# Fewer, larger loads and stores at both ends of an attention backward kernel, a deferred half load, and another cut of GpSimd's 2 MB

## The chip, the cores and the metric

The kernel runs on one core of a Trainium2 chip. The metric is the device time of one execution in microseconds (us), lower is better. The core has a matrix engine (TensorE, "PE" in the profile; its weight loads are "PEld"), a vector engine (VectorE, "DVE"), a scalar engine (ScalarE, "ACT"), GpSimd ("POOL") and SyncE ("SP"). Data moves between HBM, the large memory, and the core's own memory by 16 DMA engines; "DMA" always means these. A transfer is requested by an instruction on SP, ACT or POOL, and the DMA engines work through the requests of each such queue in order.

## The reference

One new query per head attends to a long cache, forward and backward, in bf16: 32 heads, 8192 keys and values of 128 numbers.

```python
q, grad_out: [1, 32, 1, 128]      k, v: [1, 32, 8192, 128]
scores = einsum('bhqd,bhkd->bhqk', q, k) * 128 ** -0.5
attn   = softmax(scores, axis=-1)
out    = einsum('bhqk,bhkd->bhqd', attn, v)
returns out, and dq, dk, dv  for the gradient grad_out of out
```

`k` and `v` are 64 MiB each and must be read once; `dk` and `dv` are as large and must be written once. All the rest is some 8 KB a tensor. With p the softmax, dV[s] = p[s] * grad_out and dK[s] = ds[s] * q, so every row of the two large outputs is a number times one row of 128.

## The kernel before, in words

Two heads make a pair; there are 16 pairs (`HP`), numbered 0 to 15. A pair's K is one tile of 128 partitions by 128 rows ("slots", `NT`) by 128 numbers: 32 KB in each partition, 4 MB in all. The same holds for V. A transfer of a whole tile has one contiguous run of 32 KB per partition; cut in two parts the runs are 16 KB, in four parts 8 KB (`rows_of`, `slots`).

There are three K tiles and two V tiles in turn (`K_BUFS`, `V_BUFS`), and results are written in place: `outer` (L294) overwrites the K tile with dK and the V tile with dV, in eight steps `r` of 16 slots, and stores them from there. So the load of K of pair j + 3 waits until dK of pair j has left the tile, and V of pair j + 2 until dV of pair j has. 

The loop over pairs (L362) does for pair j: blocks of K are transposed on DVE (L196) and multiplied on PE (L206) into scores; the maximum and the sum are taken across partitions through small PE products (L432, L446); ScalarE makes `p_rep` (L457). Then V is turned by PE (`T_ps`, L223), copied by ACT (L228) and multiplied with grad_out (L240), p is contracted with V (L273), and DVE writes dV (L298). dK of the pair before is done in the same stretch: its `ds` at L327 to L339, its contraction (L273) and its eight steps of `outer`. For pairs 0 to 2 and after pair 15 the order is a little different (`early`, `ends`).

The order of instructions on every engine is the order of the program text (`manual_schedule`, L134). All large transfers are requested on SP except one: the first half of dV of pair 0 (slots 0 to 63, 2 MB) is requested on GpSimd, from `share_out` (L124), once the fourth step of `outer` for that tile is done. The order of SP's requests is: K0, V0, K1, V1, K2; the second half of dV0 (L307); dK0; then in turn V of pair j + 1 (L412, L474), dV of pair j, K of pair j + 2 (L499), dK of pair j. How many parts a transfer has is read from tables: `LOADS` (L26) for loads, `PARTS` and `SPLIT` (L18, L19) for stores.

`share_out` cuts GpSimd's 2 MB by partitions: a piece `(engine, first, n)` holds n partitions in steps of three, 16 KB each. The code keeps a count of where the next GpSimd transfer will start among the 16 DMA engines (`cursor`): it takes a piece of n rows to go to as many engines as the largest divisor of n up to 16, in turn from the count on. `turn_to` (L115) puts a tiny transfer ahead of a piece, to move the count to the engine that the piece names. So `SHARES` (L28) sets how many of the 128 rows each DMA engine carries. `mark` (L108) requests 15 transfers on SP, of 1 to 15 rows of 4 bytes; they carry nothing that is used.

Of the kernel before, what the change touches and what calls it, by code (L numbers as in the profile page):

```python
# [11 lines left out]
BF16 = mybir.dt.bfloat16  # L12
# [2 lines left out]

XK_BUFS = 3
EARLY = 3
PARTS = {("dk", -1): 4, ("dv", -1): 2, ("dk", -2): 2}  # L18
SPLIT = 4  # L19
CH = 16  # L20
TB = 4
R = 4
K_BUFS = 3
V_BUFS = 2
QD = 32
LOADS = {("k", 0): 4, ("v", 0): 4, ("v", 1): 4, ("k", 2): 2, ("v", -1): 4}  # L26
SHARED = 64
SHARES = ((11, 0, 8), (6, 2, 39), (6, 1, 39), (12, 119, 3), (15, 24, 25), (5, 118, 4), (7, 99, 10))  # L28
GP = 4


# [1 line left out]
def kernel(  # L33
# [12 lines left out]
    P = 128  # L46
    _, H, S, D = k.shape
    assert D == P and (2 * S) % (P * CH) == 0 and H <= P and H % 2 == 0
    HP = H // 2
    M = P // 2  # L50
    NT = 2 * S // P
# [10 lines left out]
    kpool = ctx.enter_context(tc.tile_pool(name="kp", bufs=K_BUFS))  # L62
# [11 lines left out]
    Kt, Vt, XK, XV, st, acc, qd = {}, {}, {}, {}, {}, {}, {}  # L74

    def rows_of(x, j, c=0, parts=1):
        L = NT // parts
        return x[0, 2 * j:2 * j + 2].rearrange("b s d -> (b s) d").rearrange("(p n) d -> p n d", p=P)[:, c * L:(c + 1) * L, :]

    def slots(X, c, parts):  # L80
        L = NT // parts
        return X[:, c * L:(c + 1) * L, :]

    def load_k(j):
        Kt[j] = kpool.tile([P, NT, D], BF16, tag="K", name="Kt")
        parts = LOADS.get(("k", j), 1)
        for c in range(parts):
            nc.sync.dma_start(slots(Kt[j], c, parts), rows_of(k, j, c, parts))

    def load_v(j):  # L90
        Vt[j] = vpool.tile([P, NT, D], BF16, tag="V", name="Vt")
        parts = LOADS.get(("v", j), LOADS.get(("v", j - HP), 1))
        for c in range(parts):
            nc.sync.dma_start(slots(Vt[j], c, parts), rows_of(v, j, c, parts))

    rows = consts.tile([H, 2, D], BF16)
    nc.scalar.dma_start(rows[:, 0, :], q.rearrange("b h s d -> (b h s) d"))
    nc.scalar.dma_start(rows[:, 1, :], grad_out.rearrange("b h s d -> (b h s) d"))
    load_k(0)
    load_v(0)  # L100
    load_k(1)
    load_v(1)
    load_k(2)

    marks = list(range(1, 16))
    marked = consts.tile([16, len(marks), 2], BF16)
# [4 lines left out]

    turned = consts.tile([17, len(SHARES), 2, 2], BF16)
    cursor = [0, 0]

    def turn_to(engine):  # L115
        n = (engine - cursor[0]) % 16
        if n:
            rows = n if n > 1 else 17
            nc.gpsimd.dma_start(turned[0:rows, cursor[1]],
                                k[0, 0].rearrange("(p n) d -> p n d", p=P)[0:rows, 0:2, 0:2])  # L120
            cursor[1] += 1
        cursor[0] = engine

    def share_out(dst, src):  # L124
        for engine, first, n in SHARES:
            turn_to(engine)
            last = first + 3 * n - 2
            nc.gpsimd.dma_start(dst[first:last:3], src[first:last:3], max_dma_last_dim=8192)
            cursor[0] = (cursor[0] + max(i for i in range(1, 17) if n % i == 0)) % 16
# [60 lines left out]
    def do_window(j):  # L190
        for t in range(2):
            nc.scalar.copy(do_win[t * M:(t + 1) * M, :, :, 6 + t], do_cols[t * M:(t + 1) * M, 2 * j:2 * j + 2, :])
# [84 lines left out]
    def gather_copy(j, which):  # L277
        if j % GP != GP - 1:
            return
        S = acc["S" + which] = small.tile([P, 4, D], F32, tag="S", name="S_" + which)  # L280
        nc.scalar.copy(S[:].rearrange("p j d -> p (j d)"), acc.pop(which)[:])
# [12 lines left out]
    def outer(j, which, r):  # L294
        x = st[j]
        G, dst = (Kt[j], out_2) if which == "dk" else (Vt[j], out_3)
        rep, row = x["ds"] if which == "dk" else x["p"], qd[j][:, 0 if which == "dk" else 1, :]
        nc.vector.tensor_tensor(  # L298
            slots(G, r, NU).rearrange("p n (a b) -> p n a b", b=R),
            slots(rep, r, NU).unsqueeze(2).to_broadcast([P, CH, D // R, R]),  # L300
            row.rearrange("p (a b) -> p a b", b=R).unsqueeze(1).to_broadcast([P, CH, D // R, R]),
            op=ALU.mult)
        if (which, j) == ("dv", 0):
            if (r + 1) * CH == SHARED:
                share_out(rows_of(dst, 0)[:, 0:SHARED, :], G[:, 0:SHARED, :])
            elif r == NU - 1:
                nc.sync.dma_start(rows_of(dst, 0)[:, SHARED:NT, :], G[:, SHARED:NT, :])  # L307
            return
        parts = PARTS.get((which, j - HP), 2 if j < SPLIT else 1)
        if r % (NU // parts) == NU // parts - 1:  # L310
            c = r // (NU // parts)
            nc.sync.dma_start(rows_of(dst, j, c, parts), slots(G, c, parts))
# [49 lines left out]
    for j in range(HP + 1):  # L362
# [30 lines left out]
        if j == 0:  # L393
            blocks(1)
            first = psT.tile([P, 512], F32, tag="T", name="first")
# [9 lines left out]
        if ends and j > 0:  # L405
            gather_copy(p_, "ds")
            if early:
                half(j, 0)
            for r in range(NU):
                outer(p_, "dk", r)  # L410
            if j + 1 < HP:
                load_v(j + 1)  # L412
# [9 lines left out]
        if not ends:  # L422
            gather_copy(p_, "ds")
            outer(p_, "dk", 0)
            outer(p_, "dk", 1)
# [51 lines left out]
        for r in range(NU):  # L477
# [15 lines left out]
                    v_scores(j, r // 4)  # L493
            outer(j, "dv", r)
        gather_copy(j, "p")
        if j + 1 < HP:
            do_window(j + 1)
        if 0 < j and j + 2 < HP:
# [36 lines left out]
```

## Time and profile before

| | |
|---|---|
| three timed runs | 634.46, 634.60, 634.86 us; median 634.6 |
| the profiled execution | 634.49 us, of which its span, first to last instruction, is 632.7 |
| busy in the span | DVE 81%, PE 73%, weight loads 39%, ACT 32%, POOL 2% |
| the DMA engines | 268.98 MB, 14068 packets, 425 GB/s over the span |
| requested on SP (q1) / on GpSimd (q0) | 266.36 MB in 13152 packets / 2.10 MB in 784 packets |
| fetching of instructions (q8, q14) | 0.41 MB and 0.09 MB, by the same 16 engines |

How to read it: an engine's busy share is over the whole span. The row of DMA digits gives, for 40 equal slices of the span, the mean busy share of the 16 DMA engines; the row GB/s what they moved. A table by windows gives the same for any stretch: in each row stand the stretch, its length, the busy time of each engine with its count of instructions, the TensorE clock that was granted, the DMA engines' mean share and their GB/s. A share can read a little over 1, since the records of neighbouring packets overlap by some nanoseconds. In a timeline, "SPq" rows are requests, not transfers: the time is that of the request. "x4" after a row means that four of a kind were merged.

### The profile page before, as it was taken

The numbers are of one execution on the slowest core, as the hardware profiler recorded it, in microseconds if no ns is written. First come the engines' busy times: TensorE is split into PE (matmuls) and PEld (weight loads), VectorE is DVE, ScalarE is ACT, GpSimd is POOL, SyncE is SP. The second block draws the span as 40 slices with busy tenths as digits, with TensorE's granted clock in tenths as the row PEclk, the third lists the DMA queues.
The fourth block names the chain that finished last, engine by engine and source line by source line (L and its number), as shares of the span: only waits on it lengthen the run. The fifth ranks groups of instructions, "written<-read, shape, count | busy, mean of one in ns | idle before, by whom it ended". The sixth has DMA issues, their size and how long they took to land.

```text
span 632.7 us, 8068 instructions
## 1 busy us (share of the span) xinstructions
PE 459.6 (73%) x3256; PEld 245.6 (39%) x3256; DVE 515.6 (81%) x654; ACT 205.1 (32%) x460; POOL 11.0 (2%) x22
## 2 busy tenths in 40 slices
PE   4787676888787788676797766967679766687770
PEld 1443343253543425233362432624336243252540
DVE  6589887989889798796978969879697886978882
ACT  2432424052342505134151330604326042150440
POOL 2030000000000000000000000000000000000000
PEclk9979979779698977788977789777898878996785
DMA  8999999999999999999999999999999999999997
GB/s 363 432 402 426 439 432 422 427 431 439 430 427 436 430 428 435 428 434 432 432 434 425 432 434 432 432 431 426 432 427 432 430 433 430 431 428 415 431 430 316
DMA packets 14068, 268.98 MB, mean 425 GB/s; under 512 B 2384, under 2 KB 2384, under 8 KB 2384
## 3 DMA queue, kind: packets, MB, share of 16 engines
q1 hardware_dynamic: 13152, 266.36, 98.4%
q0 software_dynamic: 784, 2.10, 0.8%
q8 instruction: 25, 0.41, 0.2%
q14 instruction: 11, 0.09, 0.0%
q10 hardware_dynamic: 96, 0.02, 0.0%
HBM read 134.24 MB, written 134.23 MB: 424 GB/s over the span
## 4 chain that ended last, share of the span: by engine, by line
DMA 63%; PE 23%; DVE 9%; ACT 3%; issue 1%; DVEq 0%; SPq 0%; ACTq 0%
DMA Vt<-in_v_dram 26%; DMA out_dram<-Vt 25%; PE T_ps L223 11%; DMA out_dram<-Kt 6%; PE s_ps L206 6%; DMA Kt<-in_k_dram 5%; PE acc_p L273 3%; DVE Vt L298 3%; DVE Kt L298 2%; ACT XV_sb L228 2%; DVE XK_sb L196 2%; PE dp_ps L240 1%; PE acc_ds L273 1%; DVE sT L213 1%; ACT e L445 0%
## 5 line engine op out<-in xcount | busy, mean ns | idle before, releaser
L206 PE MATMUL s_ps<-XK_sb,q_win 128*128 128x512 bf16 x512 | 153.6, 438 | 65.8 <-DVE XK_sb L196 61.1
L298 DVE TENSOR_TENSOR Vt<-p_rep,qd 128x2048 bf16<-128x2048 bf16 x128 | 153.6, 1222 | 39.0 <-PE acc_p L273 29.0
L196 DVE STREAM_TRANSPOSE XK_sb<-Kt 128x1024 f32<-128x1024 f32 x128 | 149.9, 1217 | 40.0 <-DMA Kt<-in_k_dram 36.4
L223 PE MATMUL T_ps<-ident_f,Vt 128*128 128x128 f32 x1024 | 165.7, 315 | 7.5 <-DMA Vt<-in_v_dram 7.5
L228 ACT COPY XV_sb<-T_ps 128x512 f32<-128x512 f32 x256 | 139.7, 589 | 83.5 <-PE T_ps L223 83.1
L298 DVE TENSOR_TENSOR Kt<-ds_rep,qd 128x2048 bf16<-128x2048 bf16 x128 | 149.5, 1214 | 3.2 <-PE acc_ds L273 2.8
L223 PEld LDWEIGHTS T_ps<-ident_f,Vt 128*128 128x128 f32 x1024 | 132.9, 162 | 44.1 <-issue 21.5
L206 PEld LDWEIGHTS <-q_win 128*128 128x128 bf16 x512 | 52.1, 111 | 155.4 <-issue 124.0
L273 PE MATMUL acc_p<-Vt,win 128*32 128x512 bf16 x512 | 54.3, 425 | 3.6 <-ACT win L263 3.6
L445 ACT ACTIVATE e<-sT,nbias 128x128 f32<-128x128 f32 x16 | 8.2, 516 | 146.4 <-DVE nbias L441 146.4
L273 PE MATMUL acc_ds<-Kt,win 128*32 128x512 bf16 x512 | 42.8, 430 | 4.6 <-ACT win L263 3.2
L273 PEld LDWEIGHTS <-win 128*32 128x32 bf16 x1024 | 22.7, 99 | 60.0 <-issue 48.2
L263 ACT COPY win<-ds 64x128 bf16<-64x128 bf16 x32 | 9.5, 296 | 110.1 <-DVE ds L334 109.9
L240 PE MATMUL dp_ps<-XV_sb,do_win 128*32 128x512 bf16 x512 | 34.3, 384 | 13.5 <-ACT XV_sb L228 13.5
L240 PEld LDWEIGHTS <-do_win 128*32 128x32 bf16 x512 | 14.3, 94 | 29.2 <-issue 22.5
L446 PE MATMUL m_ps<-rs,ones_f 128*128 128x1 f32 x32 | 7.6, 305 | 24.4 <-ACT e L445 24.4
L432 PE MATMUL m_ps<-ident_f,top 128*128 128x128 f32 x16 | 4.8, 300 | 23.5 <-DVE top L430 23.5
L213 DVE STREAM_TRANSPOSE sT<-s_ps 128x512 f32<-128x512 f32 x16 | 11.5, 717 | 10.2 <-PE s_ps L206 10.2
L446 PEld LDWEIGHTS m_ps<-rs,ones_f 128*128 128x128 f32 x32 | 6.2, 242 | 27.6 <-ACT e L445 27.6
L457 ACT ACTIVATE p_rep<-e,rinv 128x512 bf16<-128x512 f32 x16 | 11.5, 722 | 13.3 <-DVE rinv L455 13.3
L432 PEld LDWEIGHTS m_ps<-ident_f,top 128*128 128x128 f32 x16 | 2.1, 133 | 31.1 <-issue 25.4
L324 PEld LDWEIGHTS m_ps<-pd,ones_f 128*128 128x128 f32 x32 | 8.8, 286 | 10.2 <-DVE prod L256 9.1
(59 smaller groups left out, 152.6 us busy)
## 6 DMA issues: line engine op xcount, KB each, us to landing
Kt<-in_k_dram SPq DMA_DIRECT2D x14, 4096.0 KB
Vt<-in_v_dram SPq DMA_DIRECT2D x13, 4096.0 KB
out_dram<-Vt SPq DMA_DIRECT2D x11, 4096.0 KB
out_dram<-Kt SPq DMA_DIRECT2D x10, 4096.0 KB
out_dram<-Kt SPq DMA_DIRECT2D x10, 2048.0 KB
out_dram<-Vt SPq DMA_DIRECT2D x9, 2048.0 KB
Vt<-in_v_dram SPq DMA_DIRECT2D x12, 1024.0 KB
Kt<-in_k_dram SPq DMA_DIRECT2D x4, 1024.0 KB
```

Of the source, the lines that this page charges most:

```text
L196: nc.vector.transpose(XK[j, u][:].rearrange("p g w i -> p (g w i)"), slots(Kt[j], u, NU).rearrange("p g d -> p (g d)").bitcast(F32))
L206: nc.tensor.matmul(st[j]["s"][:], lhsT=q_win[:, c, at:at + P], rhs=cols[:, c // 2, c % 2], start=(u == 0 and c == 0), stop=(u == NU - 1 an ...
L213: nc.vector.transpose(sT[:].rearrange("p g r -> p (g r)"), x["s"][:])
L223: nc.tensor.transpose(T_ps[:, i, :], words[:, m * P:(m + 1) * P], ident_f[:])
L228: nc.scalar.copy(XV[j][:, b * TB:(b + 1) * TB, :], st[j].pop(("T", c))[:])
L240: nc.tensor.matmul(out[b * QD:(b + 1) * QD, :], lhsT=do_win[:, b // 2, e2, at:at + QD], rhs=cols[:, z, e2, :, b * QD:(b + 1) * QD], start= ...
L263: nc.scalar.copy(win[t * M:(t + 1) * M, :, at:at + 4], src[t * M:(t + 1) * M])
L273: nc.tensor.matmul(acc[which][b * QD:(b + 1) * QD, :], lhsT=win[:, g, at:at + QD], rhs=X[:, 4 * g:4 * g + 4, :].rearrange("p n d -> p (n d)"),
L298: nc.vector.tensor_tensor(slots(G, r, NU).rearrange("p n (a b) -> p n a b", b=R), slots(rep, r, NU).unsqueeze(2).to_broadcast([P, CH, D // ...
L324: nc.tensor.matmul(x["m"][:, 1:3], lhsT=ones_f[:], rhs=x["pd"][:], start=True, stop=True, skip_group_check=True)
L446: nc.tensor.matmul(x["m"][:, 0:1], lhsT=ones_f[:], rhs=rs[:], start=True, stop=True, skip_group_check=True)
L457: nc.scalar.activation(x["p"][:], e[:].unsqueeze(2).to_broadcast([P, NT, R]), ACT.Copy, scale=rinv[:])
```

## The change

- Loads: K0 in two parts where it was four; V0 and V15 whole where they were four. V1 stays in four, K2 in two.
- Stores: dK0, dK1, dK3, dV2, dV3 whole where they were two halves, dK14 whole where it was two, dK15 in two where it was four. dV1, dV15 and dK2 stay in two. All others were whole and are.
- The second half of K2 is requested on SP behind the second half of dV0, where it was ahead of it. The first half stays where it was.
- GpSimd's 2 MB: again seven pieces, with other sizes, engines and order.

```diff
-PARTS = {("dk", -1): 4, ("dv", -1): 2, ("dk", -2): 2}
-SPLIT = 4
+PARTS = {("dk", 15): 2, ("dv", 15): 2, ("dv", 1): 2, ("dk", 2): 2}
...
-LOADS = {("k", 0): 4, ("v", 0): 4, ("v", 1): 4, ("k", 2): 2, ("v", -1): 4}
+LOADS = {("k", 0): 2, ("v", 1): 4, ("k", 2): 2}
 SHARED = 64
-SHARES = ((11, 0, 8), (6, 2, 39), (6, 1, 39), (12, 119, 3), (15, 24, 25), (5, 118, 4), (7, 99, 10))
+SHARES = ((15, 0, 25), (5, 75, 14), (5, 117, 4), (6, 2, 39), (7, 1, 40), (1, 119, 3), (6, 121, 3))
...
-    def load_k(j):
-        Kt[j] = kpool.tile([P, NT, D], BF16, tag="K", name="Kt")
+    def load_k(j, first=0, last=None):
         parts = LOADS.get(("k", j), 1)
-        for c in range(parts):
+        if first == 0:
+            Kt[j] = kpool.tile([P, NT, D], BF16, tag="K", name="Kt")
+        for c in range(parts)[first:last]:
             nc.sync.dma_start(slots(Kt[j], c, parts), rows_of(k, j, c, parts))
...
-        parts = LOADS.get(("v", j), LOADS.get(("v", j - HP), 1))
+        parts = LOADS.get(("v", j), 1)
...
-    load_k(2)
+    load_k(2, 0, 1)
...
-        parts = PARTS.get((which, j - HP), 2 if j < SPLIT else 1)
+        parts = PARTS.get((which, j), 1)
...
         gather_copy(j, "p")
+        if j == 0:
+            load_k(2, 1)
         if j + 1 < HP:
             do_window(j + 1)
```

By the code's own count, the rows of 16 KB that GpSimd's pieces give to DMA engines 0 to 15 are:

| engine | 0 | 1 | 2 | 3 | 4 | 5 | 6 | 7 | 8 | 9 | 10 | 11 | 12 | 13 | 14 | 15 |
|---|---|---|---|---|---|---|---|---|---|---|---|---|---|---|---|---|
| before | 13 | 12 | 12 | 5 | 0 | 1 | 7 | 8 | 8 | 7 | 7 | 8 | 9 | 9 | 9 | 13 |
| after | 13 | 10 | 10 | 6 | 0 | 2 | 6 | 10 | 10 | 8 | 8 | 8 | 8 | 8 | 8 | 13 |

## The prediction

> **What bounds the kernel now.** I read the page's busy row first, then the DMA rows, then the chain, and last the end of the span in narrow windows.
>
> ```profile
> PE 459.6 (73%) x3256; PEld 245.6 (39%) x3256; DVE 515.6 (81%) x654; ACT 205.1 (32%) x460; POOL 11.0 (2%) x22
> ...
> DMA  8999999999999999999999999999999999999997
> GB/s 363 432 402 426 439 432 422 427 431 439 430 427 436 430 428 435 428 434 432 432 434 425 432 434 432 432 431 426 432 427 432 430 433 430 431 428 415 431 430 316
> ...
> q1 hardware_dynamic: 13152, 266.36, 98.4%
> q0 software_dynamic: 784, 2.10, 0.8%
> q8 instruction: 25, 0.41, 0.2%
> ...
> DMA 63%; PE 23%; DVE 9%; ACT 3%; issue 1%; DVEq 0%; SPq 0%; ACTq 0%
> ```
>
> No engine is full, but the DMA engines read 9 in every slice except the first and the last. The chain passes through PE and DVE, yet the transfers it would hurry are always queued behind others. So the time is the bytes over the rate, plus a start, plus an end. The end, in the answer by windows:
>
> ```profile
> 620.00:625.00 5.00, 0.00 (x0) 0.00 (x0) 0.22 (x1) 0.00 (x0) 0.00 (x0) 0.50 1.00 423
> 625.00:627.00 2.00, 0.00 (x0) 0.00 (x0) 0.00 (x0) 0.00 (x0) 0.00 (x0) 0.50 1.01 426
> 627.00:628.00 1.00, 0.00 (x0) 0.00 (x0) 0.00 (x0) 0.00 (x0) 0.00 (x0) 0.50 0.84 349
> 628.00:629.00 1.00, 0.00 (x0) 0.00 (x0) 0.00 (x0) 0.00 (x0) 0.00 (x0) 0.50 0.55 226
> 629.00:630.00 1.00, 0.00 (x0) 0.00 (x0) 0.00 (x0) 0.00 (x0) 0.00 (x0) 0.50 0.29 118
> 630.00:631.00 1.00, 0.00 (x0) 0.00 (x0) 0.00 (x0) 0.00 (x0) 0.00 (x0) 0.50 0.06 19
> ```
>
> The last column but one is the DMA share. All engines work until 627, then they stop one after another. The shares add up to 1.74 us after 627: the mean engine stops at 628.7, the last at 630.75, and the span ends at 632.7. Only the last one counts. Two things can change the time: what all sixteen do (part sizes), and how evenly they stop (GpSimd's pieces).
>
> The rate by part size, also by windows:
>
> ```profile
> 6.00:22.00 16.00, 10.74 (x45) 4.58 (x45) 11.59 (x21) 1.85 (x8) 0.00 (x0) 1.00 1.01 422
> ...
> 200.00:550.00 350.00, 259.99 (x1823) 138.12 (x1823) 289.16 (x363) 113.69 (x251) 0.00 (x0) 0.83 1.00 431
> 570.00:586.00 16.00, 12.42 (x65) 4.29 (x65) 13.51 (x19) 0.59 (x2) 0.00 (x0) 0.70 0.98 418
> ```
>
> The first (K0, V0) and the third (mostly V15) move runs of 8 KB, the middle one runs of 32 KB: 422 and 418 against 431 GB/s.
>
> **The change, part by part.** The trace also holds each DMA packet's start, duration and size. On one engine a packet starts 3 to 4 ns before the one before it ends, which lets me chain the packets into sixteen engines; L110's transfers of 1 to 15 rows leave every chain a different number of tiny packets, and I number the engines by that count.
>
> *Fewer parts.* Start to start, a 32 KB packet takes 1209 ns, 16 KB 607, 8 KB 306 in stores; a part ends with a 4-byte packet of 5 ns. Each engine carries 8 packets per part. Four parts made one save 8 x (4 x 306 - 1209) + 3 x 5 ns = 0.13 us; two made one 0.04; four made two 0.09. With V0 and V15 (0.13 each), K0 and dK15 (0.09 each) and six tensors from two to one (0.26) that is 0.7 us per engine. By the windows a 4 MB tensor takes 4.19 MB/422 = 9.94 us in 8 KB runs and 9.73 at 431: 0.21 for one in four made whole, and with half and a third of that for the others, 0.42 + 0.2 + 0.4 = 1.0 us. V0's four parts finished 2.49 us apart, 9.97 us in all, against 9.68 for eight 32 KB packets: 0.29. So the bounds are 0.7 and 1.2, and I take **1.05**, since three of the four quartered tensors are loads, the slower kind. This lies on every DMA engine and so on the end.
>
> The Trainium skill's page "DMA: Bandwidth & Descriptors" (Anatomy of one DMA) fits a DMA as about 2.0 us plus bytes over 436 GB/s; taken as a toll for each request, sixteen fewer would give 32 us. The trace disagrees, since V0's quarters landed 2.49 us apart, data included.
>
> *GpSimd's pieces.* A row of 16 KB is two 8 KB packets, 0.61 us of one engine. By the chains the engines' last packets end at: 627.4 (three engines: 2, 8 and one of 7, 13, 14), 627.8 and 627.9 (0, 15), 628.5 to 628.8 (3, 5, 6, 9, 10), 629.5 (4), 629.8 and 629.9 (two of 7, 13, 14), 630.2 and 630.3 (11, 12), 630.75 (1). Where two chains end within a nanosecond they can be swapped, so 7, 13 and 14, and 1, 3, 4, 11 and 12, are sure only as groups. Within them I go by the load: 1 has 12 rows, three fetches and 2.5 us of slow packets, and 11 to 14 have 8 or 9 rows and three instruction fetches of about 1 us each since 70 us, while 7 has 8 rows and none, like 8, which stopped at 627.4. So I take 7 for early and 13 and 14 for late.
>
> With the new rows (0.61 each): 1 goes to 629.5 (two fewer), 12 to 629.7, 13 and 14 to 629.2, 7 and 8 to 628.6 (two more), 3 and 5 to 629.4; 4 (none before or after) stays at 629.5 and 11 (8 rows before and after) at 630.17. The last is 11, **0.58 us** earlier than before. If 7 is the late one it goes to 631.1, +0.35. At best all would stop with 4, which has no rows to give: -1.2. Bounds -1.2 and +0.6 (3 late at 630.75 and given a row).
>
> *Cost taken as nothing, and its cover.* K0 in halves: the first block waits for 2 MB in place of 1, 2.5 us; before, the scores of pair 0 ended at 19.6 and DVE still waited on PE, and the last of K0 landed at 12.7, so some 0.3 us remain. V0 whole: the first row below turned V0 at 21.12; V0's last packet ended at 22.64, so this starts at about 23.0 and L446, behind it on PE, runs at 24.1 in place of 22.47. dV0 with its requests moves by about 1.6 us, GpSimd's from 30.33 to 32. Cover: by then 19 MB in after (21 before) are requested ahead, enough until 46.
>
> ```profile
> 21.12 1.04 PE L223 MATMUL T_ps<-ident_f,Vt 128*128 128x128 f32 x8
> 22.47 0.38 PE L446 MATMUL m_ps<-rs,ones_f 128*128 128x1 f32 x2 [0.31 <-ACT e L445]
> ...
> 590.44 1.95 PE L223 MATMUL T_ps<-ident_f,Vt 128*128 128x128 f32 x8
> ```
>
> V15 whole: turned from 590.44 on, while its last packet ended at 591.26; 0.3 us for the signal makes it 1.1 us late at most. dV15 and dK15 move by as much. Cover at the end: the windows move 3.68 MB after 620.00. At 620.25, when the last quarter was requested, 2.5 MB stood ahead of it; with the third quarter now part of the last request, 1.47 MB do, 3.5 us; a request takes 1.0 us to its first packet (0.74 to 1.77 at the start). So 2.4 us are left, and beyond them each us costs one. At dK15's first half, now requested at 615.7, the same sum leaves 2.1; at dK14, whole at 595.7, 2.8.
>
> K2's second half: on SP's queue dV0's second half moves ahead of 2 MB, nothing else is passed, and SP itself waits no longer, since the half's buffer is free. dV0 then leaves the V tile some 5 us earlier by SP, and GpSimd's last piece (landed near 60) sets the request of V2, at about 62 in place of 65.94.
>
> ```profile
> 36.92 0.35 SPq L307 DMA_DIRECT2D out_dram<-Vt  x1
> 46.50 4.87 SPq L312 DMA_DIRECT2D out_dram<-Kt  x2
> 65.94 0.34 SPq L94 DMA_DIRECT2D Vt<-in_v_dram  x1
> ```
>
> That buys nothing: at 65.94 some 6 us of work still stood in the queue, and V2 comes behind the same bytes. Pair 2 needs the half at 79, and it lands by about 65. On GpSimd both versions have 13 transfers.
>
> *Sum*: 634.49 (profiled) - 1.05 - 0.58 = 632.86; that execution is 0.11 under the median, so **633.0** against 634.6, -0.25%. A measurement of this kernel tells about 0.2% (1.27 us) from no change.
>
> **Rivals.**
> (a) *Even end not reached*: engine 7, 3 or 5 is the last, or 1 doesn't gain. The chains allow it; the count of rows and fetches speaks against it. Price +0.35 in place of -0.58, and 0.7 to 1.05 saved: 633.8 to 634.3, within 0.2%. The Trainium skill, on the same page (Latency and other measured facts), has DMA engines 7 and 15 as usually slower; by that rule two more rows on 7 would make it the last. The trace agrees only in part: 15 stopped at 627.9 with 13 rows, and the slowest packets were 4's.
> (b) *Slower: GpSimd's own queue.* It has few transfers in flight (before, it stood 1.6 and 3.3 us for an earlier piece to land); the new order puts the 25-row piece (20.7 us to land before) first, and the 40-row piece waits behind it. If dV0's last piece lands at about 70 in place of 60, V2's request comes after the queue has run dry: from then on each us costs one, and at 74 it is +3, so some 636. Against it: engines 0 and 15 carry 13 rows in both versions, and they set the last landing.
> (c) *A toll per request*: sixteen fewer requests give far more than the packets say. V0's 2.49 us speak against it: under 0.1 us each; the most the rows allow is 1.2 us in all, inside the likeliest case's range.
> (d) *Nearly even*: 1, 11 and 12 all come down to 4's level and 1.2 us are saved: 632.1.
>
> **How the numbers follow.** The forecast case (632.4 to 633.4) 0.44; (d) 0.08; (a) 0.34; (b), with a late last pair as its smaller companion, 0.13; (c) 0.01. Faster by over 0.2% is the forecast, (d) and (c), less a little of its edge at 633.33: 0.5; within 0.2%: 0.37; slower: 0.13. The range goes from 631.9, under (d), to 635.0, above (a), and leaves out (b).
>
> **What would show it.** Right: windows of the last 8 us with all engines busy to within 2.5 us of the last packet, no share under 0.95 between 30 and 620, V2's request at 60 to 64, L446 of pair 0 about 1.6 us later. Wrong: a dip of the DMA share at 62 to 75 (b), or a staircase at the end as long as before (a); if all engines stop more than 1.3 us earlier or less than 0.6, the price of the parts was misjudged.

## The result, and the profile after

The changed kernel takes 643.88 us (median of six runs, 641.63 to 646.98) where the kernel before takes 634.9: a ratio of 1.0143, 95% interval 1.0107 to 1.018. The forecast was 633.0; the change is 9 us slower, not 1.6 faster. The profiled execution took 646.98, its span is 645.2 us, 12.5 more than before. All ratios here leave out executions in the slow state, over 1.5% longer than the fastest of the same kernel; that is a single one, of 647.38 us, in a run below.

From the page of the changed kernel, the DMA rows in 40 slices of 16.1 us, and the queues:

```profile
DMA  9999699999999999999999999999999999999996
GB/s 379 418 411 397 253 392 444 425 426 436 424 427 440 428 423 436 430 431 432 432 431 430 433 428 432 433 428 434 434 427 434 435 428 430 435 428 430 394 397 275
...
q0 software_dynamic: 816, 2.10, 0.9%
```

The fifth slice, 64.5 to 80.7 us, moves 253 GB/s in place of some 430. The last three are low too, where before only the last one was. In between, from 97 to 597 us, the two kernels move about the same.

The dip by windows (last columns: DMA share, GB/s), and SP's requests around it:

```profile
65.00:70.00 5.00, 2.32 (x17) 1.73 (x17) 4.75 (x10) 1.84 (x5) 0.00 (x0) 0.98 1.01 431
70.00:75.00 5.00, 4.36 (x31) 1.97 (x32) 3.98 (x5) 2.76 (x7) 0.00 (x0) 0.50 0.59 246
75.00:80.00 5.00, 4.60 (x41) 2.71 (x40) 5.00 (x5) 2.52 (x6) 0.00 (x0) 0.84 0.39 111
```

```profile
41.49 0.35 SPq L307 DMA_DIRECT2D out_dram<-Vt  x1
55.52 0.34 SPq L312 DMA_DIRECT2D out_dram<-Kt  x1
78.13 0.33 SPq L94 DMA_DIRECT2D Vt<-in_v_dram  x1
78.56 2.35 SPq L312 DMA_DIRECT2D out_dram<-Vt  x2
```

V2 is requested at 78.13 in place of 65.94. SP waits 22 us for it, and both stores of dV1 stand behind it on SP. The waits of SP's queue (in total, times, longest) say for what:

```profile
SPq L94 <- DMA out_dram<-Vt: 91.4, 13, 22.0
```

It is a store of a V tile. SP's half of dV0 is not it, since by the trace's signals it had landed at 60.4: the last signal of GpSimd's last piece of dV0 came at 77.9 us. Before, it was the other way round: GpSimd's last piece had landed at 61.0, and V2's request waited for SP's half, which landed at 65.8. GpSimd's requests start late and then stand still (second row: GpSimd idle for 6.22 us until an earlier piece had landed):

```profile
34.91 0.67 POOL L128 DMA_DIRECT2D out_dram<-Vt  x1 [30.79 <-DVE Vt L298]
...
46.29 1.30 POOL L128 DMA_DIRECT2D out_dram<-Vt  x2 [6.22 <-DMA out_dram<-Vt]
```

They started at 30.33 before. What made them late, from the rows of DVE and PE: the scores of pair 0 end at 21.9 (19.60 before), and V is turned at 23.46 without a wait. First the row before, then the two of the changed kernel:

```profile
19.60 0.72 DVE L213 STREAM_TRANSPOSE sT<-s_ps 128x512 f32<-128x512 f32 x1 [1.12 <-PE s_ps L206]
```

```profile
21.93 0.72 DVE L213 STREAM_TRANSPOSE sT<-s_ps 128x512 f32<-128x512 f32 x1 [1.12 <-PE s_ps L206]
```

```profile
23.46 1.04 PE L223 MATMUL T_ps<-ident_f,Vt 128*128 128x128 f32 x8
```

So 2.3 us of the 4.6 are there with the scores. The rest goes with the clock that PE was granted between 25 and 30 us, about half in this execution; the kernel before had all of it (column before the DMA share; first before, then changed):

```profile
25.00:30.00 5.00, 4.60 (x52) 2.80 (x48) 4.70 (x4) 3.78 (x9) 0.00 (x0) 1.00 0.99 426
```

```profile
25.00:30.00 5.00, 4.14 (x24) 2.35 (x24) 2.36 (x4) 3.75 (x9) 0.00 (x0) 0.54 0.97 419
```

All runs of this document taken together bear that out. From the row L213, the end of the scores of pair 0, to GpSimd's start it is 10.7 us in seven profiled executions that had the full clock there and did not wait for V0, and 12.8 to 13.0 us in the four, this one among them, that had 0.50 to 0.59 of it.

One more thing is read from the packet records. Sixteen minus the packets in flight gives the idle engines. In the changed kernel one engine has nothing to do from 69.5 us on, two from 69.75, seven at 73, eleven at 75, all from 77.5; not before 79.95 do all work again. So the engine that runs dry first loses some 10 us there, of the 12.5 that the span grew by, while the mean engine loses 5.8.

### The profile page after: what moved, and what is told of

It is laid out like the page before. It is cut to its first block, busy times and chain, and to the rows that moved or that the text cites. A ratio compares the mean times of both kernels' runs of the same rounds, so it can differ in the third digit from the quotient of the medians.

```text
span 645.2 us, 8032 instructions
## 1 busy us (share of the span) xinstructions
PE 462.8 (72%) x3256; PEld 247.4 (38%) x3256; DVE 516.2 (80%) x654; ACT 205.5 (32%) x460; POOL 11.1 (2%) x22
## 4 chain that ended last, share of the span: by engine, by line
DMA 60%; PE 24%; DVE 9%; ACT 3%; issue 2%; DVEq 0%; SPq 0%; ACTq 0%
DMA Vt<-in_v_dram 38%; DMA out_dram<-Vt 20%; PE T_ps L223 14%; PE acc_p L273 4%; DVE Kt L298 3%; PE s_ps L206 3%; DVE Vt L298 2%; ACT XV_sb L228 2%; PE dp_ps L240 2%; DVE XK_sb L196 2%; DMA Kt<-in_k_dram 1%; PE acc_ds L273 1%; ACT win L263 0%; DVE sT L213 0%; ACT p_rep L457 0%
## 5 line engine op out<-in xcount | busy, mean ns | idle before, releaser
L206 PE MATMUL s_ps<-XK_sb,q_win 128*128 128x512 bf16 x512 | 155.2, 441 | 72.5 <-DVE XK_sb L196 66.2
L223 PE MATMUL T_ps<-ident_f,Vt 128*128 128x128 f32 x1024 | 168.2, 318 | 11.4 <-DMA Vt<-in_v_dram 11.3
L223 PEld LDWEIGHTS T_ps<-ident_f,Vt 128*128 128x128 f32 x1024 | 134.4, 163 | 49.1 <-issue 25.4
L273 PE MATMUL acc_p<-Vt,win 128*32 128x512 bf16 x512 | 56.5, 444 | 3.4 <-ACT win L263 3.4
L273 PEld LDWEIGHTS <-win 128*32 128x32 bf16 x1024 | 22.7, 98 | 59.8 <-issue 47.7
L273 PE MATMUL acc_ds<-Kt,win 128*32 128x512 bf16 x512 | 40.8, 412 | 4.6 <-ACT win L263 4.6
L213 DVE STREAM_TRANSPOSE sT<-s_ps 128x512 f32<-128x512 f32 x16 | 11.5, 717 | 11.3 <-PE s_ps L206 11.3
```

Source lines behind the costliest of these rows:

```text
L206: nc.tensor.matmul(st[j]["s"][:], lhsT=q_win[:, c, at:at + P], rhs=cols[:, c // 2, c % 2], start=(u == 0 and c == 0), stop=(u == NU - 1 an ...
L213: nc.vector.transpose(sT[:].rearrange("p g r -> p (g r)"), x["s"][:])
L223: nc.tensor.transpose(T_ps[:, i, :], words[:, m * P:(m + 1) * P], ident_f[:])
L273: nc.tensor.matmul(acc[which][b * QD:(b + 1) * QD, :], lhsT=win[:, g, at:at + QD], rhs=X[:, 4 * g:4 * g + 4, :].rearrange("p n d -> p (n d)"),
```

## The experiments

Theory L, formed on this profile: the loss hangs on when GpSimd's last piece lands. V2 overwrites dV0's tile, so its request waits for that landing; and while it waits, SP's queue runs dry. The landing is late for two reasons. GpSimd starts later; and on each DMA engine its packets take turns with SP's, so that a turn costs it 0.3 us for its own 8 KB packet and then the length of one packet of SP's, 0.3, 0.6 or 1.2 us for 8, 16 or 32 KB. The rivals: theory E, the loss is made at the end, by uneven engines and late stores; theory K, the deferred half of K2 empties the queue.

The turns themselves can be read from the packet records, chained into sixteen engines as in the prediction. In the changed kernel, between 40 and 70 us, exactly one packet of SP's lies between one packet of GpSimd's and the next in 582 of 637 cases. Start to start, such a turn takes 0.61, 0.91 or 1.5 us for an 8 KB packet of GpSimd's beside 8, 16 or 32 KB of SP's. And only 256 of GpSimd's 816 packets carry rows of dV0: the other 560 have 4 to 136 bytes and take turns all the same, at 0.31, 0.61 or 1.2 us each. So the size of SP's packets counts for more than the bytes of GpSimd's suggest.

### The old loads at the start

```diff
-LOADS = {("k", 0): 2, ("v", 1): 4, ("k", 2): 2}
+LOADS = {("k", 0): 4, ("v", 0): 4, ("v", 1): 4, ("k", 2): 2}
```

> The changed kernel with the loads of the start as before: K0 and V0 in four parts each. Theory L (the loss hangs on when GpSimd's last piece of dV0 lands: V of pair 2 is requested only then, at 78.1 us, after SP's queue ran dry at about 71): GpSimd gets its rows at about 30.5 in place of 34.9, so some 7 more of its packets go in turn with the 8 KB packets of V1 and not with 32 KB ones, the landing moves to about 67, the queue does not run dry, and the run is 634 to 637. Theory E (the loss is made at the end, by engines that stop unevenly and stores that come late): 641 to 646, as the changed kernel. Theory K (the deferred half of K2 leaves too little in SP's queue): 641 to 646.

Measured: 635.9 us, ratio to before 1.0015 (1.0005 to 1.0024). GpSimd starts at 31.46, its last piece lands at 66.4, and V2 is requested at 66.62; no engine is idle for more than 0.1 us between 64 and 84 us. Theory L holds, E and K fall as explanations of the bulk. From SP's requests in this run, as above:

```profile
66.62 0.33 SPq L94 DMA_DIRECT2D Vt<-in_v_dram  x1
```

### K0 alone in four parts again

```diff
-LOADS = {("k", 0): 2, ("v", 1): 4, ("k", 2): 2}
+LOADS = {("k", 0): 4, ("v", 1): 4, ("k", 2): 2}
```

> The changed kernel with K0 in four parts again, V0 still whole. If K0's halves are what delays the first half of dV0 (the scores of pair 0 end 2.3 us later; V0 had landed at 22.4 and the turning at 23.5 did not wait for it): 635 to 637, as with both undone. If V0 whole is: 641 to 646. In the prediction V0 was the later of the two; here it would be V0 that delays, to some 32 us, and V2's request would come at about 68: 637 to 639.

Measured: 636.57 us, 1.0048 (1.0019 to 1.0077); GpSimd at 31.55, as in the run above. So it is K0 in halves that delays the hand-over most. V0 whole adds a little once K0 is in four: the turning of V (L223) waited 1.03 us for V0 here and began at 22.89, and from the end of the scores to GpSimd's start it was 11.4 us in place of 10.7. Beside K0 in halves this doesn't show, since the scores come later than V0 anyway. The ten timed executions lie between 635.78 and 647.38. V2's request came at 67.69 in the profiled one, close to where the first engine goes idle in other runs, at 67 to 69.5 us. That the long executions are those in which a slightly later hand-over fell over that edge fits, but only one of the ten was profiled.

### dK0 in two halves again

```diff
-PARTS = {("dk", 15): 2, ("dv", 15): 2, ("dv", 1): 2, ("dk", 2): 2}
+PARTS = {("dk", 0): 2, ("dk", 15): 2, ("dv", 15): 2, ("dv", 1): 2, ("dk", 2): 2}
```

> The changed kernel with dK of pair 0 stored in two halves, so that GpSimd's last packets take turns with 16 KB packets in place of 32 KB ones between 60 and 75 us. Theory L: the last piece lands some 4 to 6 us earlier (72 to 74), the dry stretch shrinks to 1 to 3 us, 637 to 641. Theories E and K: 641 to 646, no change.

Measured: 639.75 us, 1.0075 (1.006 to 1.009). The last piece lands at 70.1, and not one of GpSimd's packets waits out a 32 KB packet, where in the changed kernel 107 do. Not all of the 4 us need be the halves': PE had its full clock at 25 to 30 us in this profiled execution, and GpSimd started at 33.41, 1.5 us earlier. Here is the reading that the prediction lacked. By the DMA share of these windows all engines work at the time in question, and only the GB/s are somewhat low:

```profile
65.00:70.00 5.00, 2.58 (x31) 1.64 (x32) 4.02 (x8) 3.21 (x8) 0.00 (x0) 1.00 0.99 419
70.00:75.00 5.00, 4.61 (x56) 2.72 (x48) 5.00 (x5) 3.54 (x8) 0.00 (x0) 1.00 1.00 398
```

and yet the span is 5.3 us longer than before. The packet records show one engine idle from 68.15 to 71.43; averaged over the sixteen, the idle time there is only 0.25 us. At the end, twelve of the sixteen chains have their last packet by 631.5 us, and a single one ends at 636.1. A mean over sixteen engines hides one that stands still, and the end waits for the last one. That the two are the same engine was not traced through the run, and 2 of the 5.3 us are not accounted for.

### dK0 whole in the kernel before

```diff
-        parts = PARTS.get((which, j - HP), 2 if j < SPLIT else 1)
+        parts = PARTS.get((which, j - HP), 2 if j < SPLIT and (which, j) != ("dk", 0) else 1)
```

> The kernel before with dK0 stored whole and nothing else. Theory L: GpSimd's last piece has landed (61 us) before dK0's packets start, so 32 KB packets have nobody to hold up: 634 to 635.5, no change, though undoing the same part of the changed kernel gained 4 us. If a whole dK0 costs by itself: 637 to 640.

Measured: 634.97 us, 1.0000 (0.999 to 1.0009). What is worth up to 4 us in the changed kernel costs nothing here: in the chains none of GpSimd's packets waits out a 32 KB packet, its last piece lands at 63.9, and V2's request, at 65.86, waits for SP's half of dV0 (65.7) as before. The parts of this change don't add up; a whole dK0 costs only together with a late hand-over.

### GpSimd's pieces as before, in the changed kernel; and the new pieces alone

```diff
-SHARES = ((15, 0, 25), (5, 75, 14), (5, 117, 4), (6, 2, 39), (7, 1, 40), (1, 119, 3), (6, 121, 3))
+SHARES = ((11, 0, 8), (6, 2, 39), (6, 1, 39), (12, 119, 3), (15, 24, 25), (5, 118, 4), (7, 99, 10))
```

> The changed kernel with GpSimd's seven pieces as before. Theory L: engines 0 and 15 carry 13 rows in both cuts, so the last piece lands about where it did (72 to 77), the dry stretch stays, 639 to 644; only if the wait of the 40-row piece for the 25-row piece is what makes the landing late does it come near 636. Theory E: the engines stop as evenly as before, 636 to 639. Theory K: 641 to 646.

Measured: 640.78 us, 1.0108 (1.0072 to 1.0145). Landing 70.9, V2 at 71.22, an engine idle for 5.7 us. In its profiled execution PE had its full clock at 25 to 30 us and GpSimd started at 33.23, so part of the gain against 643.88 need not be the pieces'. The reverse edit, in the kernel before:

> The kernel before with the new seven pieces and nothing else. Theory L: handed over at 30.3 us, both cuts land in time (V2's request waits for SP's half of dV0, at 64.5), so only the evenness of the end differs: 634.2 by the prediction's table of engines (engine 11 last, -0.6), 635.0 to 637 if the new cut makes the end less even, as the 2.9 us of idle engine time at the end of the changed kernel with the old start loads suggest against 1.9 before.

Measured: 635.5 us, 1.0010 (1.0001 to 1.0019). The new cut lands in time (63.3) and makes the end not more even but, if anything, less: +0.65 us where the prediction's table gave -0.58.

### K2 requested whole at the start again

```diff
-    load_k(2, 0, 1)
+    load_k(2)
...
-        if j == 0:
-            load_k(2, 1)
```

> The changed kernel with all of K2 requested at the start, as before. Theory K: V2 is requested before the queue runs dry, 634 to 636. Theory L: the same bytes stand ahead of V2 in either order and GpSimd's turns are with 16 KB packets in either order, so the dry stretch stays, 641 to 646. Theory E: 641 to 646.

Measured: 643.93 us, 1.0143 (1.0117 to 1.0169), the same as the changed kernel. Theory K falls.

### The hand-over delayed in the kernel before

The first form moved only the text:

```diff
-            if (r + 1) * CH == SHARED:
+            if r == NU - 1:
                 share_out(rows_of(dst, 0)[:, 0:SHARED, :], G[:, 0:SHARED, :])
-            elif r == NU - 1:
```

> The kernel before with one edit: GpSimd gets its half of dV0 after the eighth step of dV and not after the fourth, at about 37 us in place of 30.3. Nothing else differs, sizes and pieces neither. Theory L (the landing of GpSimd's last piece sets V2's request, and the engine with the least in its queue goes idle from 68 us on until V2 comes): some 10 turns are lost beside 8 KB packets and made up beside 16 KB ones, the landing goes from 61 to about 71, V2's request from 65.9 to about 71, one engine idles about 4 us, and the run is 638 to 641. Rival E (the loss of the changed kernel came from its pieces and its late stores): 634.5 to 635.5, no change.

Measured: 634.84 us, 1.0002 (0.9993 to 1.0011): nothing was tested. GpSimd had nothing else to do and its transfers wait for the slots that they read, so they started at 30.95 as before. The second form gives GpSimd a copy of two numbers that come last:

```diff
+                seen = consts.tile([P, 2], BF16, name="seen")
+                nc.gpsimd.tensor_copy(seen[:], G[:, NT - 1, 0:2])
                 share_out(rows_of(dst, 0)[:, 0:SHARED, :], G[:, 0:SHARED, :])
```

> The kernel before, with one small GpSimd copy of two numbers from the last slot of dV0 put ahead of GpSimd's half, so that its requests start at about 37.5 us in place of 30.5 (the edit before this one moved them only in the text). Pieces, sizes and order are those of before. Theory L: some 11 turns beside 8 KB packets are lost and made up beside 16 KB ones (0.9 us each), the last piece lands at 69 to 72 in place of 61, V2 is requested then, the first engine idles 2 to 5 us, and the run is 636.5 to 640. Rival E: 634.5 to 635.5.

Measured: 644.49 us, 1.0153 (1.014 to 1.0166), more than was expected, and as slow as the changed kernel, with none of its edits. GpSimd starts at 38.95, lands at 76.2, and V2 follows:

```profile
76.55 0.34 SPq L94 DMA_DIRECT2D Vt<-in_v_dram  x1
```

So the delayed hand-over alone suffices; a start 8.6 us later moved the landing by 15.2. Hardly any of GpSimd's turns were beside 8 KB packets here (2, and 583 beside 16 KB), where the kernel before had 375 and 243.

### Smaller parts beside GpSimd, in the changed kernel

```diff
-LOADS = {("k", 0): 2, ("v", 1): 4, ("k", 2): 2}
+LOADS = {("k", 0): 2, ("v", 1): 4, ("k", 2): 4}
-PARTS = {("dk", 15): 2, ("dv", 15): 2, ("dv", 1): 2, ("dk", 2): 2}
+PARTS = {("dk", 0): 4, ("dk", 15): 2, ("dv", 15): 2, ("dv", 1): 2, ("dk", 2): 2}
...
-                nc.sync.dma_start(rows_of(dst, 0)[:, SHARED:NT, :], G[:, SHARED:NT, :])
+                for c in (2, 3):
+                    nc.sync.dma_start(rows_of(dst, 0, c, 4), slots(G, c, 4))
...
-    load_k(2, 0, 1)
+    load_k(2, 0, 2)
...
-            load_k(2, 1)
+            load_k(2, 2)
```

> The changed kernel with the transfers that run beside GpSimd's pieces cut smaller: K2 in four parts, the second half of dV0 in two, dK0 in four, so that SP's packets there are 8 KB in place of 16 and 32 KB. That is six parts more, some 0.4 us of work more. Theory L: a turn costs GpSimd 0.6 us in place of 0.9 to 1.5, the last piece lands at 60 to 65 in place of 78, V2's request follows, no engine idles, 635 to 638. If larger parts are better as such, or the loss lies elsewhere: 642 to 647.

Measured: 636.14 us, 1.0021 (1.0012 to 1.003). This kernel starts GpSimd late (32.81), keeps the new pieces and the deferred half, and moves more and smaller packets; yet it gets back 7.7 of the 9 us:

```profile
36.71 3.05 SPq L308 DMA_DIRECT2D out_dram<-Vt  x2
46.72 9.10 SPq L313 DMA_DIRECT2D out_dram<-Kt  x4
61.38 0.34 SPq L94 DMA_DIRECT2D Vt<-in_v_dram  x1
```

Its last piece lands at 59.8, 18 us earlier than in the changed kernel from a start only 2.1 us earlier. What differs beside GpSimd's packets is the size of SP's: in the chains all of its turns are beside 8 KB packets. A start as early does not do it, as two runs above show, which started at 33.2 and 33.4 and landed at 70.9 and 70.1. That GpSimd's packets take turns with SP's is what the Trainium skill states too: its page "DMA: Bandwidth & Descriptors" (Queues, rings and completion order) has each DMA engine go round the queues that have work, packet by packet. The trace agrees, in the 582 of 637 cases above and in what follows from it, the landing at 59.8 beside 8 KB packets.

### The later parts merged in the kernel before, and an attempt at a better one

```diff
-PARTS = {("dk", -1): 4, ("dv", -1): 2, ("dk", -2): 2}
-SPLIT = 4
+PARTS = {("dk", 0): 2, ("dk", 15): 2, ("dv", 15): 2, ("dv", 1): 2, ("dk", 2): 2}
...
-LOADS = {("k", 0): 4, ("v", 0): 4, ("v", 1): 4, ("k", 2): 2, ("v", -1): 4}
+LOADS = {("k", 0): 4, ("v", 0): 4, ("v", 1): 4, ("k", 2): 2}
...
-        parts = PARTS.get((which, j - HP), 2 if j < SPLIT else 1)
+        parts = PARTS.get((which, j), 1)
```

> The kernel before with only those parts merged that lie after GpSimd's pieces: dK1, dK3, dV2, dV3, V15 and dK14 whole, dK15 in halves. By the prediction's term this saves 0.4 to 0.8 us on every DMA engine: 634.0 to 634.4. If the later requests of dK14 and dK15 leave an engine without work at the end, as the dips at 605 to 610 and 625 to 630 in the changed kernel hint: 635 to 636.5.

Measured: 634.73 us, 0.9994 (0.9985 to 1.0002). If there is a saving it is some 0.4 us, at the lower end of what was expected, and it can't be told from none. The next kernel adds to this:

```diff
-LOADS = {("k", 0): 4, ("v", 0): 4, ("v", 1): 4, ("k", 2): 2}
+LOADS = {("k", 0): 4, ("v", 1): 4, ("k", 2): 2}
-SHARES = ((11, 0, 8), (6, 2, 39), (6, 1, 39), (12, 119, 3), (15, 24, 25), (5, 118, 4), (7, 99, 10))
+SHARES = ((11, 0, 8), (6, 2, 39), (6, 1, 39), (7, 119, 3), (15, 24, 25), (5, 118, 4), (7, 99, 10))
```

> The kernel of the run above, with V0 whole too and one piece of three rows of before moved from engines 12 to 14 to engines 7 to 9. V0 whole does not delay the hand-over by the runs so far, and saves 0.1 to 0.3 us. In the runs with the pieces of before, the chains of packets of engines 12 to 14 ended at 630.1 and those of 7 and 8 at 27.1 us after 600, so the end comes 0.3 to 0.6 us earlier: 633.2 to 634.0 if all terms hold; over 634.8 if the end runs dry.

Measured: 639.08 us, 1.0058 (1.0038 to 1.0078), with executions from 634.33 to 641.54. It fell over the same edge. GpSimd started at 33.75 in the profiled execution: PE had half its clock at 25 to 30 us, and V was turned 1.17 us late, waiting for V0 whole. And the moved piece no longer ends where the 25-row piece begins, so one more tiny transfer is put between them, and GpSimd requests the 25 rows 6.55 us after its start (at 40.30), where before it was 4.05 us (at 34.38). The last piece lands at 69.5, and an engine is idle from 66.9 to 70.8. Which of the three was decisive was not tested. No version here is shown to be faster than the kernel before.

### All runs side by side

From each kernel's profiled execution, in us. "Landed" is the last signal of GpSimd's last piece. "Turns" counts, in the chains, how often exactly one packet of SP's lies between two of GpSimd's, by the size of SP's packet, 8, 16 or 32 KB. "Idle" is the longest stretch between 64 and 84 us in which fewer than sixteen packets were in flight, so that at least one DMA engine had none.

| kernel | GpSimd starts | turns 8 / 16 / 32 KB | landed | V2 requested | idle | span |
|---|---|---|---|---|---|---|
| before | 30.33 | 375 / 243 / 0 | 61.0 | 65.94 | 0.0 | 632.7 |
| before, text moved | 30.95 | 351 / 268 / 0 | 62.2 | 66.01 | 0.0 | 632.9 |
| before, dK0 whole | 31.93 | 293 / 326 / 0 | 63.9 | 65.86 | 0.1 | 633.1 |
| before, later parts merged | 32.68 | 258 / 359 / 0 | 65.8 | 66.33 | 0.0 | 633.2 |
| before, new pieces | 31.03 | 329 / 309 / 0 | 63.3 | 65.92 | 0.0 | 633.7 |
| changed, old start loads | 31.46 | 299 / 329 / 0 | 66.4 | 66.62 | 0.1 | 633.9 |
| changed, smaller parts beside | 32.81 | 590 / 0 / 0 | 59.8 | 61.38 | 0.0 | 634.1 |
| changed, K0 in four | 31.55 | 281 / 354 / 0 | 67.4 | 67.69 | 0.5 | 634.4 |
| the attempt at a better one | 33.75 | 200 / 469 / 0 | 69.5 | 69.69 | 3.8 | 636.9 |
| changed, dK0 halves | 33.41 | 205 / 440 / 0 | 70.1 | 70.32 | 3.3 | 638.0 |
| changed, old pieces | 33.23 | 215 / 359 / 30 | 70.9 | 71.22 | 5.7 | 639.0 |
| changed, K2 at the start | 34.46 | 146 / 360 / 107 | 75.8 | 76.06 | 9.2 | 643.2 |
| before, hand-over delayed | 38.95 | 2 / 583 / 0 | 76.2 | 76.55 | 8.8 | 643.2 |
| changed | 34.91 | 131 / 368 / 107 | 77.9 | 78.13 | 10.5 | 645.2 |

Up to a request of V2 at about 67 the time hardly depends on it. Beyond, each us costs one: from 67.69 to 78.13, 10.4 us, the span grows by 10.8. In the runs past that edge the span follows the longest idle stretch and not the mean one: with dK0 in halves and with the old pieces the mean engine was idle for 0.25 and 0.9 us, and the spans grew by 5.3 and 6.3.

## Why the prediction was wrong

*What bounds the kernel*: right. The DMA engines do, and only the engine that stops last counts. This second half was then not used where it mattered.

*Cost taken as nothing, K0 in halves*: wrong. "Some 0.3 us remain" was 2.3: the first block of K waits 2.5 us longer, and almost none of that was made up by the end of the scores. (In all profiled executions the scores end at 19.1 to 20.8 with K0 in four and at 21.7 to 22.7 with K0 in halves.) Of the variants of the changed kernel with the full clock at 25 to 30 us, the three with K0 in halves start GpSimd at 32.8 to 33.4, the two with K0 in four at 31.5.

*V0 whole*: priced at 1.6 us of delay, too much. In the changed kernel V0's last packet ended at 22.4, in time for scores that were themselves later; with K0 in four V was waited for, and the hand-over came 0.6 us later.

*K2's half, and V2's request "at about 62"*: here the prediction failed. SP's half did leave the V tile some 5 us earlier, as it said (60.4 for 65.8). But it took GpSimd's landing, near 60, from before and moved it by nothing, and costed dK0 whole at a saving of 0.04 us. The price of a part was asked for the tensor that is merged and not for GpSimd's packets, which wait out SP's packets in turn. GpSimd's last piece landed at 77.9, and V2's request came at 78.1. The half of K2 itself was costed at nothing, which is right.

*"At 65.94 some 6 us of work still stood in the queue"*: wrong in kind. That was the mean over sixteen engines. The engine with the least work runs dry at 67 to 69.5 in the runs above, some 1 to 3.5 us after the 65.94 of before, and a request needs about 1 us itself to its first packet (78.13 to 79.09 in the changed kernel). So the kernel before has little cover there. That it is an engine with few of GpSimd's rows (4 has none, 5 has one or two) follows from the table of rows and was not shown by a run.

*Fewer parts, -1.05*: not confirmed. Seven of the ten tensors gave -0.4 us, with an interval from -1.0 to +0.1, which holds both nothing and the 0.4 to 0.8 that the term gives for these seven.

*GpSimd's pieces, -0.58*: wrong sign, +0.65 alone (+0.1 to +1.2). Engine 7, whose place was open, was indeed early: in the run with the text moved the chains of 7 and 8 ended at 627.1 and 627.2, those of 12 to 14 at 630.1. But the rows moved did not carry the ends as the table said; with the new cut, chains 12 and 13 ended at 631.9 and 630.8, with a row less. Why is open. The numbers of these chains carry the prediction's own doubt: two that end within a nanosecond can be swapped.

*Engines 7 and 15*: that the Trainium skill, page "DMA: Bandwidth & Descriptors" (Latency and other measured facts), has them as usually slower was drawn on in rival (a). The same run puts 7 at 627.1 and 15 at 628.2, among the early ones, so far as the numbering holds. The trace doesn't agree here.

*Cover at the end*: it held for the kernel before with the merged stores. In the changed kernel the DMA share falls to 0.57 at 606 to 608, while dK14, whole, is requested at 607.89. The window there:

```profile
606.00:608.00 2.00, 2.00 (x12) 1.57 (x8) 2.00 (x3) 0.89 (x2) 0.00 (x0) 0.50 0.57 246
```

It goes with the idle stretch at 70 and not with the merged stores by themselves. With the old start loads, which leaves these stores as they are, every 5 us from 590 to 625 reads 0.96 to 1.01, while the kernel before with the hand-over delayed, which has the old stores, falls to 0.91 at 620 to 625. The runs with the same stores and no idle stretch come to within 1.2 to 1.7 us of the span before. Whether the whole dK14 makes the dip deeper was not tested.

*Rival (b)*, given 0.13, is nearest to what happened: its place, the wait for an earlier piece (6.22 us) and the price of a us for each us late were right. Its cause, the new order of the pieces, was at most a part: with the pieces of before the changed kernel still took 640.78. Its size, some 636, was too small, since the landing came at 78 and not 74 and the first engine ran dry sooner. It was held unlikely since "engines 0 and 15 carry 13 rows in both versions, and they set the last landing": the number of rows was the same, the length of a turn was not.

## What to carry to other kernels

Where two queues share the DMA engines, price a larger part not only on its own queue: it lengthens each turn of the other queue, and if a load waits for the other queue's last landing, that wait grows. Count the cover of a late request for the engine with the least queued, not for the mean; a profile whose windows of 5 us all show 0.99 or 1.00 can have one engine idle, and if all must finish, that engine's loss is the kernel's. And undo each part of a bundle in the changed kernel as well as trying it alone in the old one: here one part cost up to 4 us in the one and nothing in the other.

## What had not been expected of the hardware

- Small requests are not small in landing time beside another queue. GpSimd's last two pieces, of 48 KB each, took 27.8 us (median) to land in the changed kernel; its tiny transfers up to 22:

```profile
out_dram<-Vt POOLq DMA_DIRECT2D x2, 48.0 KB, 27.8
turned<-in_k_dram POOLq DMA_DIRECT2D x1, 0.0 KB, 22.1
```

- The granted PE clock at 25 to 30 us differs from one profiled execution to the next, 0.50 to 1.00, in variants of either kernel. It read 1.00 in the kernel before, and 0.59 and 0.51 with dK0 whole and with the later parts merged, whose program is the same up to there; this cost some 2.1 us of the hand-over and nothing of the time. In the changed kernel it read 0.54, and there it adds to a hand-over that is already at the edge. That this is what spreads the changed kernel's six runs over 5.3 us was not shown.
